# A new hand-written order for all engines, a second group of rows kept in DRAM, a first segment cut in two, and pooled sums on two engines

## The chip, the cores and the metric

One core of a Trainium2 chip runs the whole program. The metric is the device time in microseconds of one execution; lower is better. Five engines work side by side, each through its own queue in program order: TensorE (PE, with its weight loads PEld), VectorE (DVE), ScalarE (ACT), GpSimd (POOL) and SyncE (SP), which issues all DMAs here.

## What is computed

Three stages over 4608 tokens (8 batches of 576) with 512 features (8 heads of 64): attention against keys and values that are averaged over groups of 8 positions, an expert with SoLU and layer norm (512 to 1024 to 512), and an expert with SiLU (512 to 2048 to 512). The two experts' weights arrive as 64-bit floats.

```python
k_p = k.reshape(B, H, 72, 8, D).mean(axis=3)
v_p = v.reshape(B, H, 72, 8, D).mean(axis=3)
scores = scale * (q @ k_p.T)
attn = exp(scores - max(scores));  attn = attn / (sum(attn) + 1e-09)
x = attn @ v_p                                   # (4608, 512)
h = x @ w_in                                     # (4608, 1024)
sm = exp(h - max(h));  solu = h * sm / (sum(sm) + 1e-09)
ln = (solu - mean(solu)) / sqrt(var(solu) + 1e-06) * g_ln
x = ln @ w_out                                   # (4608, 512)
h = x @ w_in2                                    # (4608, 2048)
out = (h / (1 + exp(-h))) @ w_out2               # (4608, 512)
```

## The kernel before

Tokens go in 36 tiles of 128. Matrix products are made from pairs of reduced-precision operands, a high part and a low part (`fp32r`), with three matmuls for each product; the projection of the first expert and both products of the second run by a seven-product scheme for 2x2 blocks (Strassen-Winograd), whose block sums and differences are made on VectorE, ScalarE and GpSimd.

**The scripted part.** Attention, the first expert and the start of the second are issued in an order that is written out by hand: `SCRIPT` (lines 61 to 216) is a string of words, and `run` (line 1462) walks through it. A word names a generator and its arguments, and each occurrence runs that generator to its next `yield`; a suffix `/1`, `/2`, `/3` puts the step on VectorE, ScalarE or GpSimd instead of its default (`pick`, line 275). As every engine works in program order, this string fixes the order of all five queues. The words are:

- `L`, `l`: load a block of w_in as 64-bit floats; turn it into 32 bits and split it (lines 1333 and 1322). The conversion (`convert`, line 287) takes two ScalarE steps, of which the second can be on VectorE, and one VectorE step (line 307). `w` (`keep_f32`, line 326) converts a block of the second expert's weights (w2) in the same way and stores it in DRAM; there are 32 blocks. `o` (line 1383) does the first expert's second matrix, with all its sums and splits, in four calls.
- `k`, `v`, `r` (lines 381, 412, 440): load rows of keys and values, sum them over 8 positions (lines 393, 425, 453, all on VectorE), then scale or split them into small operand tiles. Loads go to three row buffers in turn.
- `q`, `S`, `X`, `T`, `a`: load a tile of queries, its scores and their maximum, the softmax (exponentials on ScalarE, products with the reciprocal on GpSimd or VectorE), transposes by TensorE and their splitting, and the attention products (`attend`, line 593). `a` works on segments of tokens: 256, 320, 320 and 256 for each two batches (`segments`, line 221).
- `H`, `M`, `E`, `Z`, `N`: hidden products of a tile (three matmuls of 512 columns each, eight words a tile), their row maximum (line 656), exponentials and sums, normalization, and transposes into a ring of six tiles (`norm_T`, line 705).
- `R`, `D`, `P`: the projection operands of a group of four tiles, the weight blocks that come from DRAM, and the seven products of the group (24 matmuls of 256 columns each), whose results go to DRAM (`x2d`). Groups are taken in the order of `LAST` (line 37): 1 to 7, then 0, then 8. Group 0's rows are normalized before the projection weights are ready; `norm_T` stores them in DRAM (`lnd`, line 722), and `u` (`reload_n`, line 725) fetches them back near the end.
- `c`, `d`: close the attention's and the hidden part's buffers and make the second expert's first tokens and weights in their place. `f` (`first_pair`, line 1058): its first seven products, 42 matmuls.

`W` issues matmuls whose result is not used.

**Behind the script** the second expert's first half runs in windows (`window`, line 1093; `product`, line 1036, matmuls at line 1043), with the conversions of its operands placed in numbered slots, and then its second half (`product2`, line 1275, matmuls at line 1286), with its operands made nine products ahead.

## Time and profile before

| | |
|---|---|
| median of 3 runs | 1294.44 us (1293.19 to 1296.17) |
| profiled execution | 1291.54 us, its span 1289.5 us |
| granted TensorE clock, mean | 0.989 |
| TensorE, VectorE, ScalarE, GpSimd busy | 96%, 79%, 62%, 36% |
| DMA | 304 MB, 236 GB/s on average |

The span runs from the first to the last instruction. A busy TensorE is not TensorE at its peak, since matmuls overlap and their ends are modelled. The granted clock tells which share of full speed the throttle allowed. The scripted part ends with the last projection at 586.7 us; the hand-over to the windows lasts to 606.2, the windows to 941 and the second half to the end. Lines are named by their number in the kernel before. In a group of instructions, `out<-in` are the program's tile names, and the figures are the sum of busy time, the mean of one in ns, and the idle time ahead of them with what ended it.

### The profile page before, as it was taken

To read this page: it belongs to the slowest core of one execution; us is meant where nothing else is said; L and a number is where in the kernel's file an instruction comes from. 1 tells how busy PE (TensorE), PEld (TensorE's weight loads), DVE (VectorE), ACT (ScalarE), POOL (GpSimd) and SP (SyncE) were. 2 spreads that over 40 slices of the span, in tenths; PEclk is the share of its full clock that TensorE was granted. 3 is DMA by queue.
4 is the path that set the end of the run, shared out by engine and by line. 5 is a ranking of instruction groups with operands and counts; after the bars stand their busy time and mean duration, and the time that the engine had idled before them with its cause. 6 is when DMAs were issued, how large, how long until landed. Compare 5 with 4: busy or idle time off the path is not lost.

```text
span 1289.5 us, 21677 instructions
## 1 busy us (share of the span) xinstructions
PE 1244.0 (96%) x7276; PEld 1134.2 (88%) x7276; DVE 1016.6 (79%) x1689; ACT 795.8 (62%) x1965; POOL 461.6 (36%) x623
## 2 busy tenths in 40 slices
PE   7788999999999999898999999999999999999999
PEld 6677778899899998898999999999988888888888
DVE  6888998998887789898766677656479887969776
ACT  6788987675465645444767677676645445554544
POOL 4777775555645645523224433333030000000000
PEclk8899999999999999999999999999999999999999
DMA  9777688766323341544778688666999988788683
GB/s 328 219 251 237 196 281 305 234 232 197 107 87 106 107 164 58 180 159 168 264 276 302 254 299 332 247 230 222 339 331 403 356 285 268 256 272 273 196 283 142
DMA packets 133167, 304.47 MB, mean 236 GB/s; under 512 B 11936, under 2 KB 56992, under 8 KB 131520
## 3 DMA queue, kind: packets, MB, share of 16 engines
q1 hardware_dynamic: 133056, 303.09, 68.1%
q8 instruction: 57, 0.93, 0.3%
q14 instruction: 54, 0.44, 0.1%
HBM read 213.91 MB, written 89.13 MB: 235 GB/s over the span
## 4 chain that ended last, share of the span: by engine, by line
PE 52%; DMA 1%; DVE 1%; issue 0%; ACT 0%; DVEq 0%; SPq 0%; ACTq 0%
PE op L1286 27%; PE m L1043 25%; DMA gd<-gb 1%; DMA w2r<-w2if 0%; DVE w2r L837 0%; PE xq L785 0%; DVE np L287 0%; DVE xo L793 0%; DVE gb L1054 0%; ACT gt L1266 0%; DVE t L837 0%; DVE wt L872 0%; DVE np L282 0%; DVE wt L837 0%; DVE w2s L837 0%
## 5 line engine op out<-in xcount | busy, mean ns | idle before, releaser
L1043 PE MATMUL m<-t,w2s 128*128 128x384 f32 x2016 | 352.6, 335 | 4.2 <-DVE gb L1054 2.1
L1043 PEld LDWEIGHTS m<-t,w2s 128*128 128x128 f32 x2016 | 350.7, 188 | 5.7 <-DVE gb L1054 2.7
L1286 PE MATMUL op<-gt,w2o 128*128 128x512 f32 (+1 forms) x1680 | 345.2, 368 | 0.0
L1286 PEld LDWEIGHTS op<-gt,w2o 128*128 128x128 f32 x1680 | 292.7, 189 | 52.4
L1266 ACT ACTIVATE gt<-gr 128x512 fp32r<-128x512 f32 (+1 forms) x240 | 139.9, 588 | 142.5 <-PE op L1286 58.9
L837 DVE TENSOR_TENSOR gt<-gr,gt 128x512 fp32r<-128x512 f32 (+1 forms) x240 | 154.6, 650 | 60.9 <-ACT gt L1266 57.4
L643 PE MATMUL hp<-w1ih,xTh 128*128 128x512 f32 x288 | 119.6, 415 | 7.3 <-DVE e L668 4.5
L785 PE MATMUL xq<-np,w1p 128*128 128x256 f32 x864 | 113.5, 284 | 1.3 <-DVE np L287 1.0
L643 PE MATMUL hp<-w1ih,xTl 128*128 128x512 f32 x288 | 114.1, 396 | 0.4 <-DVE xTl L287 0.4
L643 PE MATMUL hp<-w1il,xTh 128*128 128x512 f32 x288 | 113.6, 394 | 0.0
L785 PEld LDWEIGHTS xq<-np,w1p 128*128 128x128 f32 x864 | 107.0, 189 | 3.9 <-DVE np L287 1.7
L513 ACT ACTIVATE pr<-sp,st 128x72 f32<-128x72 f32 x288 | 88.2, 329 | 23.2 <-DVE st L504 19.2
L785 PE MATMUL xq<-np,w1o 128*128 128x256 f32 x648 | 86.7, 286 | 5.1 <-DVE np L287 3.7
L785 PEld LDWEIGHTS xq<-np,w1o 128*128 128x128 f32 x648 | 81.8, 192 | 7.8 <-DVE np L287 4.1
L287 POOL TENSOR_TENSOR np<-lnr,np 128x512 fp32r<-128x512 f32 x46 | 62.2, 1356 | 49.7 <-DVE np L282 28.8
L837 DVE TENSOR_TENSOR gr<-gr 128x512 f32<-128x512 f32 (+1 forms) x120 | 79.8, 667 | 0.2
L837 POOL TENSOR_TENSOR tt<-x2r 128x768 f32<-128x768 f32 x22 | 43.5, 1979 | 99.3 <-DMA x2r<-x2d 60.4
L643 PEld LDWEIGHTS hp<-w1ih,xTh 128*128 128x128 f32 x288 | 55.1, 191 | 18.3 <-DVE e L668 3.4
L287 DVE TENSOR_TENSOR np<-lnr,np 128x512 fp32r<-128x512 f32 x80 | 64.6, 815 | 4.4 <-ACT np L280 2.7
L666 ACT ACTIVATE e<-hp,ls 128x1024 f32<-128x1024 f32 x36 | 40.1, 1115 | 45.2 <-DVE ls L656 40.4
L643 PEld LDWEIGHTS hp<-w1ih,xTl 128*128 128x128 f32 x288 | 54.7, 190 | 13.3 <-DVE xTl L287 1.0
L280 ACT ACTIVATE np<-lnr 128x512 fp32r<-128x512 f32 x69 | 43.0, 630 | 36.1 <-PE xq L785 18.0
(177 smaller groups left out, 2225.7 us busy)
## 6 DMA issues: line engine op xcount, KB each, us to landing
w2o<-wod SPq DMA_DIRECT2D x50, 768.0 KB, 6.5
w1o<-w1od SPq DMA_DIRECT2D x54, 512.0 KB, 4.2
...
```

Of the source, the lines that this page charges most:

```text
L280: eng.activation(dst, src, AF.Copy)
L287: pick(1).tensor_tensor(lo, src, hi.bitcast(F32), op=ALU.subtract)
L513: nc.scalar.activation(pr[:, g, h], sv[:, g, h], AF.Exp, bias=st[:, 0, g, h : h + 1], accum_out=st[:, 1, g, h : h + 1],)
L643: nc.tensor.matmul(hp[:, f], l, r, start=(n == 1 and m == 0), stop=(n == KC and m == 2))
L666: nc.scalar.activation(e, hp, AF.Exp, bias=nm, accum_out=sm)
L785: nc.tensor.matmul(hq[:, b], w[:, k, l], t[:, k % 2, r], start=(b == k == i == 0), stop=(k == 3 and i == 2), skip_group_check=True,)
L837: eng.tensor_tensor(dst, a, b, op=ALU.subtract)
L1043: nc.tensor.matmul(to, wt[:, a, o : o + P], tk[:, b, k], start=(start and k == 0 and m == 0), stop=(k == 1 and m == 2), skip_group_check=n ...
L1266: nc.scalar.activation(ring[m][:, 0], src, AF.Copy)
L1286: nc.tensor.matmul(acc[c, x][d], w[:, l, P * d : P * d + P], t[:, r], start=(first and f == i == 0), stop=(f == NF - 1 and i == 2), skip_g ...
```

## The change

1. `SCRIPT` is a new string, all words from first to last in a new order, with 2881 instead of 2859 words. Of the 32 w2 conversions (`w`), 27 were begun ahead of tile 15's row maximum and the last ahead of tile 19's; now 15 are begun ahead of tile 15's and the last ahead of tile 30's. The key loads come earlier in the opening. The `f` words stand behind the last projection matmul; two of their seven products stood ahead of it.
2. `SPILL = 2`: group 1 is treated as group 0 was. Its rows go to DRAM (four stores of 0.52 MB more), are fetched back by two reloads of 1.05 MB more, and `LAST` takes it fourth: 2, 3, 4, 1, 5, 6, 7, 0, 8. The first projection is that of group 2, behind hidden tile 12 instead of tile 11.
3. The first segment of 256 tokens is two of 128. In the order the attention products of the first (`a0`) stand behind tile 0's transposes and ahead of tile 1's.
4. `pool_sum` lets a word put a pooled sum on GpSimd, as three halving adds in place; 19 of the 80 sums are there. `scaled` and `pick` do the same for the scaling and the splitting of pooled keys and values, which can now be on any of three engines.

```diff
-LAST = (1, 2, 3, 4, 5, 6, 7, 0, 8)
+SPILL = 2
+LAST = (2, 3, 4, 1, 5, 6, 7, 0, 8)
...
 SCRIPT = """
-L0,1 L0,0 W14 L0,2 k0,0 v0,0 k0,2 L0,3 q0 l0,1 L1,0 l0,1 l0,1 W29 l0,1 l0,0 l0,1 l0,2 q1
-l0,0 l0,0 k0,0 L1,1 l0,0/3 k0,1 k0,1 k0,1 v0,0 v0,2 k0,0 k0,0 l0,2/1 W6 l0,2 v0,1 l0,2/3
-r0,0 W4 k0,3 l0,2/3 k0,2 l0,3 L1,3 l0,3/1 k0,3 l0,3 k0,3 k0,2 L1,2 k0,2 S0 k1,0 l0,0 l0,3 S0
...
-R8,2 P8,2 N34 R8,5 d P8,2 P8,1 D8,4,0 R8,6 f R8,6 D8,4,1 R8,6 R8,6/3 R8,6 f f P8,2 R8,6/3 d
-P8,6 P8,2 f R8,4 d P8,6 R8,7 P8,5 P8,6 R8,7/1 d d P8,5 D8,2,0 R8,7 R8,7/3 R8,7 d R8,7 P8,7
-R8,3/1 D8,2,1 R8,3 R8,3 P8,5 R8,3/3 P8,7 P8,3 P8,7 P8,7 R8,4/1 P8,3 R8,4 R8,4/3 R8,4/1 R8,4
-P8,4 d d d P8,4 P8,3 P8,3 f P8,4 d P8,4 f f f f f f f f f f f
+L0,0 k0,0 W14 L0,2 k0,2 q0 L0,1 q1 q6 W6 l0,0 L0,3 W29 k0,0 k1,0 l0,0/1 k0,1 l0,2 k0,1/3
+k0,1/1 l0,0 l0,2/1 k0,0/1 k0,0 l0,2 k0,2 l0,2 k0,3 k0,2 k0,2/1 k0,3/1 k0,3/3 S0 l0,1 S0 q2
+k1,1 S1,1 l0,0/1 X0 v0,0 l0,1/1 v0,2 l0,2 X0 W4 r0,0 S1,1 L1,3 X0 X0 l0,0 v1,0 X1 l0,1 X1
...
+N35 R8,2 P8,2 R8,5 R8,6/3 P8,2 D8,4,0 R8,6 D8,4,1 R8,6 R8,6/3 R8,6 d R8,6 P8,6 P8,1 c P8,6
+R8,7 d P8,2 P8,5 R8,7 d P8,2 c d P8,5 d D8,2,0 R8,7/3 R8,7 P8,6 R8,7 R8,3 D8,2,1 R8,7 P8,7 d
+d d d P8,7 R8,4 R8,3 R8,3 R8,3 P8,3 R8,4 R8,4/3 R8,4 P8,5 R8,4 P8,3 d R8,4 P8,4 P8,7 P8,7
+P8,4 P8,3 P8,3 f P8,4 d P8,4 f f d d f f f c f f f f f f f f f f
 """
...
-        for a, n, b in ((0, 256, 0), (256, 320, 0), (576, 320, 1), (896, 256, 1)):
+        first = ((0, 256, 0),) if j else ((0, 128, 0), (128, 128, 0))
+        for a, n, b in first + ((256, 320, 0), (576, 320, 1), (896, 256, 1)):
...
-    lnd = [dram.tile([P, FC1, 2 * P], F32, tag=f"lnd{h}", name="lnd") for h in range(2)]
+    lnd = [dram.tile([P, FC1, 2 * P], F32, tag=f"lnd{h}", name="lnd") for h in range(2 * SPILL)]
...
+    def pool_sum(dst, raw):
+        if pick(1) is nc.vector:
+            nc.vector.reduce_sum(dst, raw, axis=AX)
+            return
+        for n in (4, 2, 1):
+            to = raw[:, :, 0:n] if n > 1 else dst.rearrange("p (k o) -> p k o", o=1)
+            nc.gpsimd.tensor_tensor(to, raw[:, :, 0:n], raw[:, :, n : 2 * n], op=ALU.add)
+
+    def scaled(n, dst, src, scale):
+        if pick(n) is nc.scalar:
+            nc.scalar.activation(dst, src, AF.Copy, scale=scale)
+        else:
+            pick(n).tensor_scalar(dst, src, scale, 0.0, op0=ALU.mult, op1=ALU.add)
...
-        nc.vector.reduce_sum(kp[:, p], raw, axis=AX)
+        pool_sum(kp[:, p], raw)
...
-            nc.gpsimd.tensor_tensor(lo, vp[r], hi.bitcast(F32), op=ALU.subtract)
+            pick(3).tensor_tensor(lo, vp[r], hi.bitcast(F32), op=ALU.subtract)
...
     def norm_T(t):
         e = v_t.pop(t)
-        o = (t if t < NTILE - GT else t + GT) % TRING * P
+        g, i = divmod(t, GT)
+        o = (t if g < SPILL else (SPILL + LAST.index(g)) * GT + i) % TRING * P
...
-        if t < GT:
+        if g < SPILL:
             nc.sync.dma_start(lnd[t // 2][:, :, t % 2 * P : t % 2 * P + P], ring_t[0][:, :, o : o + P])
...
-    def reload_n(h):
-        o = (NTILE - GT + 2 * h) % TRING * P
-        nc.sync.dma_start(ring_t[0][:, :, o : o + HW], lnd[h])
+    def reload_n(g, h):
+        o = ((SPILL + LAST.index(g)) * GT + 2 * h) % TRING * P
+        nc.sync.dma_start(ring_t[0][:, :, o : o + HW], lnd[2 * g + h])
```

## Rows read from the trace of the kernel before

**Rows 1.** The page's part 1: busy us (share of the span) xinstructions, by engine.

```profile
PE 1244.0 (96%) x7276; PEld 1134.2 (88%) x7276; DVE 1016.6 (79%) x1689; ACT 795.8 (62%) x1965; POOL 461.6 (36%) x623
```

**Rows 2.** The chain that ended last, in time: start us, us, what.

```profile
588.58 6.14 DMA w2r<-w2if
...
606.17 316.86 PE m L1043 x1818
...
941.29 345.00 PE op L1286 x1680
```

**Rows 3.** Windows: stretch, length, busy (x) PE PEld DVE ACT POOL, PEclk, DMA share, GB/s.

```profile
0.00:52.10 52.10, 37.06 (x230) 33.13 (x230) 38.61 (x65) 35.35 (x134) 26.43 (x44) 0.90 0.85 285
52.10:182.00 129.90, 114.63 (x620) 94.42 (x620) 116.23 (x226) 110.93 (x399) 98.36 (x190) 0.96 0.75 239
182.00:332.50 150.50, 148.62 (x1031) 136.18 (x1032) 135.94 (x246) 100.56 (x292) 87.13 (x131) 1.00 0.68 228
332.50:478.20 145.70, 145.19 (x984) 132.93 (x983) 118.64 (x212) 79.29 (x250) 83.01 (x126) 1.00 0.35 111
...
535.00:586.70 51.70, 47.29 (x372) 45.97 (x372) 46.75 (x69) 22.26 (x38) 17.03 (x17) 0.97 0.54 172
586.70:606.20 19.50, 15.44 (x87) 14.48 (x85) 13.77 (x16) 7.91 (x16) 8.26 (x5) 0.99 0.60 212
```

**Rows 4.** Timeline, VectorE: row maxima of tiles 0 and 11: start us, us, instruction.

```profile
52.14 1.22 DVE L656 TENSOR_REDUCE ls<-hp 128x1 f32<-128x1024 f32 x1
...
182.03 1.23 DVE L656 TENSOR_REDUCE ls<-hp 128x1 f32<-128x1024 f32 x1
```

**Rows 5.** Windows as in rows 3: first and last half-clock stretch ahead of 605 us.

```profile
22.20:29.10 6.90, 5.37 (x25) 5.35 (x26) 5.96 (x12) 5.41 (x21) 4.80 (x6) 0.51 1.04 393
...
544.40:548.00 3.60, 2.97 (x14) 3.00 (x15) 2.50 (x4) 3.41 (x6) 3.33 (x5) 0.53 0.23 90
```

**Rows 6.** Groups by line and form, and line 307's spread (ns min/median/max).

```profile
L307 DVE SCALAR_TENSOR_TENSOR w<-w,tail 128x512 int32<-128x512 int32 x48 | 38.5, 803 | 9.7 <-ACT tail L303 8.8 <-ACT w L299 0.3
L307 DVE SCALAR_TENSOR_TENSOR w<-w,tail x48: 672/691/2650, 6.0 to 356.0; 128x512 int32<-128x512 int32 x48
L393 DVE TENSOR_REDUCE kp<-raw 128x72 f32<-128x576 f32 x28 | 20.7, 745 | 4.7 <-DMA raw<-kT 3.9 <-POOL kbd L406 0.8
L425 DVE TENSOR_REDUCE vp<-raw 128x64 f32<-128x512 f32 x28 | 18.6, 673 | 3.1 <-DMA raw<-vm 3.1
L287 DVE TENSOR_TENSOR xTl<-av,xTh 128x128 fp32r<-128x128 f32 x24 | 6.0, 279 | 0.9 <-ACT xTh L280 0.9
L287 DVE TENSOR_TENSOR np<-lnr,np 128x512 fp32r<-128x512 f32 x80 | 64.6, 815 | 4.4 <-ACT np L280 2.7 <-POOL np L284 0.8
L287 DVE TENSOR_TENSOR ptl<-pm,pth 128x512 fp32r<-128x512 f32 x32 | 21.9, 686 | 0.6 <-ACT pth L280 0.2
L689 POOL TENSOR_TENSOR ls<-ls 128x1 f32<-128x1 f32 x36 | 10.6, 294 | 2.8
L525 POOL TENSOR_TENSOR pb<-pr,st 128x512 f32<-128x512 f32 x24 | 25.8, 1074 | 25.2 <-DVE st L521 23.2 <-ACT kbd L402 1.8
```

**Rows 7.** Timeline of the opening: the last key sums, first scores, first hidden product.

```profile
13.24 1.40 DVE L393 TENSOR_REDUCE kp<-early 128x72 f32<-128x576 f32 x2
...
15.38 1.15 PE L494 MATMUL sp<-kbd,q 128*128 128x144 f32 x8
...
38.79 0.50 PE L643 MATMUL hp<-w1ih,xTh 128*128 128x512 f32 x1 [2.55 <-ACT xTh L280]
```

**Rows 8.** Waits: engine, line, releaser: us in total, times, longest us.

```profile
DVE vlp L453 <- DMA raw<-vl: 4.9, 3, 3.5
...
SPq L722 <- ACT lnr L280: 6.0, 1, 6.0
```

**Rows 9.** Timeline, VectorE and GpSimd from 33 to 36 us.

```profile
33.24 2.65 DVE L307 SCALAR_TENSOR_TENSOR w<-w,tail 128x512 int32<-128x512 int32 x1
...
34.07 1.27 POOL L287 TENSOR_TENSOR w1il<-w,w1ih 128x512 fp32r<-128x512 f32 x1
```

More of the change, by code (lines that the diff above doesn't have):

```diff
@@ new lines @@
+E18 D4,1,1 Z18 Z18 H19,0,0 N17/1 N17 P3,3 H19,0,1 w20 R4,1/1 P3,3 w16 T23 R4,1 H19,1,0 X26
+w16/1 R4,1/1 X26 T23 w21 H19,0,2 w16 r5,1/2 R4,1/3 w19 N17/1 H19,0,3 w16 w19 r6,1 k7,3
+H19,1,1 X26 r5,1 w22 H19,1,2 R3,4 X26 w19 H19,1,3 X26 R3,4/3 T23 P4,1 M19 v6,3 Z18 X26 S27
+X25 E19 T23 R3,4/3 P3,4 Z18/2 q30 E19 X26 w19 u1,0 N16 P3,4 w20/1 k7,3/2 v6,3 T23/1 w23 T23
+v7,0 X26 T24 w20 H20,0,0 E19 P3,4 Z19 Z19 T24 H20,1,0 X25/1 H20,1,1 w21 S27 Z19 H20,1,2
+T24/1 P4,1 R4,2/1 Z19/2 k7,3 T24 r6,0 r6,1/3 X27 N18 T24/1 v6,3 v7,1 N19 T24 X25 v7,2
@@ new lines @@
+D1,1,0 R4,7/3 R4,7 w24 r7,0 H22,0,0 w25 R1,1 R4,7/3 H22,1,0 E21 R4,7 Z21 Z21 P4,7 S29 P4,5
+Z21 P4,7 R1,1 r6,1/1 a11 v7,3/3 Z21/2 P4,7 H22,1,1 a11 H22,0,1 Z20/2 P4,3 R4,4/3 a11 a11 a11
+R1,1/3 H22,1,2 a11 a11 H22,0,2 H22,1,3 H22,0,3 R4,4 R4,4/3 R1,1/3 R4,4 w22 N20 w26 T25
+R4,4/3 P4,7 T25 T25/1 P4,4 T25 T25 u1,1 P4,3 w22 D1,1,1 X27 M22 w22 q32 N20/1 N20 P4,4 N20
+E22 P1,1 P4,4 X28 P4,4 X28/1 N21 X28 T26 E22 N21 P1,1 R1,2/1 E22 R1,2 R1,2 Z22 T26 H23,0,0
+R1,2 H23,1,0 X27 T25 w24 T26/1 P1,2 X29 R1,5 Z22 T26 R1,5 H23,0,1 T26/1 X29 D1,4,0 R1,5
@@ new lines @@
+R6,5/3 a14 M28 N27 R6,5/3 S35 N27 a14/1 E28 a14 a14 R6,6/3 a14 S35 P6,5 E28 X35 X35 P6,5
+a14/1 D6,2,0 E28 a14 R6,7/3 Z28 X34 a14 a14 D6,2,1 Z28 R6,6/1 H29,1,0 a14 T31/1 R6,3 Z28
+H29,1,1 w28/1 T31 X35 H29,1,2 w28 X35 R6,3 T32 H29,0,1 H29,0,0 R6,6/3 R6,6 R6,4 R6,6 a14
+H29,1,3 T32 T32 R6,3 T32 H29,0,2 T32 X35 R6,6/3 w30 T32 H29,0,3 X35 T31/1 T31 T33 M29 Z28
+T33 P6,6 T33/1 R6,3/3 T33 T33 E29 P6,6 E29 P6,3 R6,7/3 P6,6 H30,0,0 R6,7/3 R6,7 P6,5 R6,7
+D7,1,0 w28 a15 H30,1,0 E29 R6,7 P6,7 w30 X35 Z29 w30 P6,7 r7,1 r7,1 Z29 H30,0,1 P6,7 R6,4
@@ new lines @@
+X34 H30,0,3 H30,1,1 Z29 R6,4 H30,0,2 T33 v7,3/1 N28 Z29 P6,3 N28 r7,1/2 X35 N28 X34 D7,1,1
+a15 N28/1 R6,4/3 N29 a15/1 N29 a15 a15 a15 H30,1,2 u0,0 R6,4/3 a15/1 P6,7 a15 a15 a15 a15/1
+a15 a15 a15 T34 H32,0,0,1 P6,3 T34 T34/1 P6,3 H30,1,3 T34 T34 T35 H32,1,0,1 M30 T35
+H32,0,1,1 T35/1 E30 H32,1,1,1 T34 T35 H32,0,2,1 T35 E30 a16 N29 H32,1,2,1 T35 E30 a16 N29/1
+Z30 Z30 H31,0,0 R6,4 a16/1 a16 a16 a16 H31,0,1 a16 a15/1 R7,1/1 a16 a16 a16 R7,1/3 R7,1
+a16/1 a16 a16 a16 H31,1,0 a16 H31,1,1 a16 Z30 a15 c H31,0,2 c c H31,0,3 H31,1,2 c H31,1,3 c
@@ L401, in prep_k @@
             if b <= 1:
-                nc.scalar.activation(
-                    kb[r, p, e * SP : (e + 1) * SP], kp[r, p], AF.Copy, scale=SCALE
-                )
-            else:
-                nc.gpsimd.tensor_scalar(
-                    kb[r, :, e * SP : (e + 1) * SP], kp[r], SCALE, 0.0, op0=ALU.mult, op1=ALU.add
-                )
+                scaled(2, kb[r, p, e * SP : (e + 1) * SP], kp[r, p], SCALE)
+            else:
+                scaled(3, kb[r, :, e * SP : (e + 1) * SP], kp[r], SCALE)
             done("k", b)
@@ L424, in prep_v @@
         vp = vp_t[b]
-        nc.vector.reduce_sum(vp[:, p], raw, axis=AX)
+        pool_sum(vp[:, p], raw)
         done("vp", b)
@@ L452, in prep_v_rest @@
         vp = vr_t[b]
-        nc.vector.reduce_sum(vp[:, g], raw, axis=AX)
+        pool_sum(vp[:, g], raw)
         done("vr", b)
@@ L466, in prep_v_rest @@
         for j in range(4):
-            nc.gpsimd.tensor_scalar(
-                vls[i][:, j // 2 :: 2, (j % 2) * D : (j % 2 + 1) * D],
-                vh.bitcast(F32), mask[:, j : j + 1], 0.0, op0=ALU.mult, op1=ALU.add,
-            )
+            to = vls[i][:, j // 2 :: 2, (j % 2) * D : (j % 2 + 1) * D]
+            scaled(3, to, vh.bitcast(F32), mask[:, j : j + 1])
             done("v", b)
```

269 lines of the change are left out of this document (124 added, 145 removed).

## The prediction, made before the result was known

> **What bounds the kernel now.** The page's first lines come first: TensorE is busy 96% of the span, VectorE 79%, ScalarE 62%, GpSimd 36% [rows 1]. The chain of work that ended last says where: from 606.2 us on it is matmuls of the second expert without a gap worth naming, 317 us of line 1043 and then 345 us of line 1286 [rows 2]. No line of that part is changed and its operands come in the same order, so the 683 us behind 606.2 stay as they are. The change can only act ahead of that point.
>
> There I read busy time by stage, cut at the row maxima of the hidden tiles (word M, line 656), since each marks the same progress in both orders [rows 3, 4]. Tile 0's maximum stands at 52.1 us, tile 11's at 182.0; tile 35's is where the stage from 535.0 begins. From tile 0 to tile 11 TensorE is busy 114.6 of 129.9 us (88%), VectorE 116.2 (89%), ScalarE 110.9 (85%), GpSimd 98.4 (76%): no engine is full, and the vector work is what the others queue behind. From 182.0 to 332.5 VectorE has 90% and TensorE 98.8%; from 332.5 to 478.2 VectorE falls to 81% and TensorE has 99.7%: there TensorE is the bound and VectorE has 27 us to spare. Behind tile 35 TensorE drops again, to 91%, and in the hand-over from 586.7 to 606.2 it idles 4.1 us.
>
> So the time is lost in the first 182 us (30.3 us of idle TensorE: 15.0 and 15.3) and at the end of the scripted part (4.4 and 4.1 us). Idle costs twice: in stretches among the gaps the granted clock is 0.51 to 0.53, the 1.2 GHz level instead of 2.4, once for 6.9 us and otherwise for about 3.5; six such stretches lie ahead of 605 us, the first and the last of which are shown, five of them in the first 122 us [rows 5].
>
> **The change, part by part.** Nearly the same instructions run; where they stand is new. I counted the words of both orders ahead of tile 11's maximum, because up to there neither order has a projection and both have the same 96 hidden products.
>
> *w2 conversions later.* Word w has run its vector step (line 307) 13 times ahead of that point before, 6 times after: seven fewer at 0.803 us are 5.6 us of VectorE [rows 6], and two ScalarE steps go with each. *Pooled sums on two engines.* VectorE has 58 of the sums ahead of that point before and 46 after: 12 at 0.71 us (the mean of 0.745 and 0.673) take off 8.5 us [rows 6]. Eleven stand on GpSimd instead, as three halving adds. The trace has no such add. From the nearest rows three adds cost between 0.9 us (three times 0.294, the smallest two-input form) and 3.2 us (three times 1.074, 128x512) [rows 6]; I take 1.9, near the middle, since their 288, 144 and 72 elements lie between. *What comes back to VectorE:* 23 small scalings and splittings of pooled keys and values that GpSimd or ScalarE had, at about 0.3 us (nearest row 0.279 [rows 6]), 6.8 us, and 0.2 of other differences. Net VectorE has 7.1 us less ahead of tile 11, 2.1 of it ahead of tile 0. GpSimd has 2.5 us more, since much that was its own is moved away. Means overstate, because neighbours overlap at their ends: my list gives 167.7 us of VectorE ahead of tile 11 where rows 3 show 154.8, so I scale by 0.92. Between tile 0 and tile 11 that is 5.0 x 0.92 = 4.6 us of work, and at a VectorE share of 89% the stage becomes **5.1 us** shorter. Bounds: 0 (the waits are chains, not load) and 10 us (twice that, if ScalarE's relief counts too).
>
> *Opening.* The first scores wait for all pooled keys of the first batch: the last two sums start at 13.24 us, the scores at 15.38 [rows 7]. Before, 3.28 MB are asked for up to and with the second key load (three blocks of w_in at 0.52, keys 0.59, values 0.52, keys 0.59), after 2.23 MB (two blocks, two key loads). 1.05 MB at 285 GB/s [rows 3] are **3.7 us**. Behind the scores the first segment is one tile, so the first hidden product, at 38.79 us before [rows 7], no longer waits for a second softmax. Against that, values are asked for later and there are 16 more attention matmuls. Bounds 0 and 6 us; I take 3.7.
>
> *Middle.* What left the first part must be done later. From tile 11 up to the place that is reached at 332.5 us now, the counted VectorE work is even (153.5 before, 151.1 after); in the stage behind it rises by 7.3 x 0.92 = 6.7 us, so from 118.6 to 125.3 of 145.7 us, 86%. At 90% TensorE idled 1.2%, at 81% 0.3% [rows 3]: the loss is 0 to 1.3 us, and I take **1.0**.
>
> *Second group through DRAM.* Four more stores of 0.52 MB in the first part and two reloads of 1.05 MB in the middle, where the DMA engines are busy 35 to 68% [rows 3]. In the first part nine w2 blocks fewer are read (0.52 MB) and written (0.26), which more than pays for the stores. SyncE's queue could suffer: a store waits for its copy, once 6.0 us before, and key, value and q loads stand behind it. There are now eight such places instead of four. VectorE waited for value rows up to 3.5 us at a time [rows 8], so this costs 0 to 3 us; I take 0, as row buffers are asked for three ahead. The reloads are asked for two tiles and half a tile ahead of their readers; 1.05 MB at 285 GB/s are 3.7 us, half a tile some 6.
>
> *End.* Behind tile 35 the two orders have 42.1 and 34.7 us of TensorE work left by my count, and vector work moves with it. No product of the first pair, instead of two, stands ahead of the last projection matmul; their twelve matmuls, at 316.86/1818 = 0.174 us, move 2.1 us of work into the hand-over, where TensorE waits for w2 rows (6.14 us to land, then sums) [rows 2] and idles 4.1. There they cost nothing; in front of it they are gained if TensorE sets the pace, and not if VectorE does. Bounds -2.1 and +1 (a later w2 load); I take **-1.0**.
>
> **A rule that speaks against it.** A vector step with a median of 0.691 us once took 2.65, with GpSimd instructions running through it [rows 6, 9]. The Trainium skill ("SBUF — State Buffer", section "Who interferes with whom") says that a vector instruction with two inputs in SBUF and a GpSimd one that reads SBUF exclude each other for a whole instruction, and that a vector reduce does not contend, so exchanging reduces for GpSimd adds would cost vector time. That one row agrees. By the rule at its worst the time would be 1306.5, by the median of the row 1285.6; the first is among the rivals.
>
> **Sum**, against the profiled execution (1291.54 us, a span of 1289.5 and 2.04 around it): -5.1 - 3.7 + 1.0 - 1.0 = -8.8, so 1282.7. The median of the runs is 2.9 us above that execution, and I put the forecast on the median: **1285.6**.
>
> **Rivals.**
> *Held vector work* (slower). If each GpSimd sum kept VectorE waiting for its whole 1.9 us, eleven of them would give back 20.9 us: 1306.5. It decides, nothing gained, from 42% of that. Against it: line 307 lies 0.112 us above its median, 5.4 us over 48, and line 287 with two SBUF inputs 0.129 above its form with one, 10.3 over 80 [rows 6]; 16 us over some 320 of GpSimd work [rows 3] are 5%, so 1 us here. Chance 0.06.
> *Middle becomes vector-bound* (slower). If the stretch from 332.5 to 478.2 ran at the 88% of the first part, its 145.2 us of TensorE work would take 165, 19 more: 1285.6 + 18 = 1304. It decides from a TensorE share of about 94%. For it: VectorE at 89% went with 88% in the first part. Against: at 90% it went with 98.8% in the next [rows 3]. Chance 0.14.
> *Larger gain.* Lighter ScalarE and VectorE let the softmax chains run with fewer gaps, so that half of the 15.3 us idle goes besides: 1278.0, and up to 1.75 us less for each half-clock stretch that goes too. Chance 0.20.
> *Given back.* VectorE's whole scripted load is the same (536.8 and 536.1 us by my count), and it ends the stage again: 1294.4. For it its 90% behind tile 35; against it its slack in the middle [rows 3]. Chance 0.15.
>
> **How the numbers follow.** Forecast 0.45, larger 0.20, given back 0.15, middle 0.14, held 0.06. What a measurement of this kernel can tell from no change is about 0.2%, 2.6 us. Faster: the forecast but for its upper edge (0.42), larger (0.20) and a little of given back: 0.64. Same: most of given back and that edge: 0.16. Slower: middle and held: 0.20. The range runs from 1274.5, the larger gain with two half-clock stretches fewer, to 1300, most of the middle rival's way.
>
> **What would show it.** Tile 0's maximum near 48 us, tile 11's near 173; first scores near 12; VectorE near 86% between 320 and 470 us with TensorE still above 98%; the last 683 us unchanged. The prediction is wrong if tile 11 comes no earlier (then chains, not load, set the first part), if TensorE idles in the middle, or if vector instructions with two SBUF inputs grow by more than 5% on average.

## The result, and the profile after

The changed kernel takes 1282.23 us in the median of 4 runs (1279.98 to 1283.69), the kernel before 1293.82 (4 runs): a ratio of 0.9907, 95% interval 0.9885 to 0.9929. The forecast was 1285.6. The profiled execution took 1281.28 us, with a span of 1279.5; that is 10.3 us less than the profiled execution before.

Part 1 of the page of the changed kernel, as in [rows 1]:

```profile
PE 1242.0 (97%) x7292; PEld 1131.2 (88%) x7292; DVE 1016.8 (79%) x1719; ACT 794.1 (62%) x1949; POOL 480.7 (38%) x655
```

VectorE's sum over the span is unchanged (1016.6 before); GpSimd has 19 us more. What changed is where the work stands. The windows of the changed kernel, cut at tile 0's, 11's and 35's maxima and the last projection as in [rows 3], and between them at 320 and 463, where TensorE has done 99% and 98% of the work (columns of its matmuls, warm-up left out) that it had done at 332.5 and 478.2 before (columns as there: stretch, length, busy and count of PE, PEld, DVE, ACT, POOL, granted clock, DMA share, GB/s); the last row is a stretch of the opening, as in [rows 5]:

```profile
0.00:50.00 50.00, 38.85 (x247) 35.17 (x247) 34.79 (x74) 30.47 (x123) 25.49 (x48) 0.86 0.80 272
50.00:168.80 118.80, 108.78 (x616) 90.41 (x617) 110.96 (x228) 106.42 (x379) 96.21 (x196) 1.00 0.69 211
168.80:320.00 151.20, 147.78 (x1001) 134.31 (x1000) 139.44 (x248) 107.35 (x332) 102.20 (x151) 1.00 0.77 251
320.00:463.00 143.00, 140.57 (x975) 128.71 (x974) 119.96 (x221) 78.69 (x224) 85.04 (x120) 1.00 0.49 156
...
534.30:575.80 41.50, 37.43 (x294) 34.95 (x293) 38.03 (x55) 21.10 (x35) 17.53 (x19) 1.00 0.45 147
575.80:594.80 19.00, 16.89 (x99) 16.57 (x97) 14.60 (x19) 8.92 (x18) 8.72 (x5) 1.00 0.61 219
26.00:40.00 14.00, 9.53 (x36) 8.46 (x37) 12.38 (x28) 9.02 (x29) 10.66 (x18) 0.51 0.87 320
```

Tile 0's row maximum comes at 50.0 us instead of 52.1, tile 11's at 168.8 instead of 182.0 [rows 4] (timeline; start us, us, instruction, in brackets the idle time ahead of it and what ended it):

```profile
168.79 1.23 DVE L669 TENSOR_REDUCE ls<-hp 128x1 f32<-128x1024 f32 x1 [0.29 <-PE hp L656]
```

So the 10.0 us of span are made up like this:

| stretch | before | after | difference | forecast |
|---|---|---|---|---|
| start to tile 0's maximum | 52.1 | 50.0 | -2.1 | -3.7 |
| tile 0's to tile 11's maximum | 129.9 | 118.8 | -11.1 | -5.1 |
| tile 11's maximum to the last projection | 404.7 | 407.0 | +2.3 | +1.0 (middle) |
| hand-over to the windows | 19.5 | 19.0 | -0.5 | -1.0 (end) |
| windows and second half | 683.3 | 684.7 | +1.4 | 0 |

Nearly everything lies between tiles 0 and 11, and there ahead of tile 5's maximum, which comes 51.8 us after tile 0's instead of 64.1; from there to tile 11's the new order takes 67.0 instead of 65.8 (windows of both halves, the kernel before first):

```profile
52.10:116.20 64.10, 56.10 (x302) 46.89 (x302) 54.00 (x107) 54.37 (x205) 51.28 (x101) 0.95 0.78 241
116.20:182.00 65.80, 58.53 (x318) 47.54 (x318) 62.23 (x121) 56.56 (x194) 47.08 (x89) 0.97 0.72 237
50.00:101.80 51.80, 47.64 (x268) 40.00 (x268) 48.53 (x98) 47.51 (x175) 43.74 (x88) 1.00 0.62 185
101.80:168.80 67.00, 61.14 (x349) 50.41 (x350) 62.43 (x131) 58.91 (x205) 52.47 (x109) 1.00 0.73 230
```

In the first half VectorE works 5.5 us less and idles 6.8 less, and some 34 matmuls, with the work of other engines that belongs to them, now stand behind tile 5; in the second half VectorE's work is the same. Over both halves VectorE works 5.3 us less (116.2 to 111.0; forecast 4.6) and idles 5.8 us less (13.7 to 7.8); TensorE's granted clock is 1.00 throughout where three stretches at the 1.2 GHz level stood before. The questions for the experiments were how much of the 11.1 us the lighter load is worth, how much the clock, and how much the order by itself; and why the opening gave little.

### The profile page after: what moved, and what is told of

It reads as the page before. It is cut to its first block, busy times and chain, and to the rows that moved or that the text cites. A ratio compares the mean times of both kernels' runs of the same rounds, so it can differ in the third digit from the quotient of the medians.

```text
span 1279.5 us, 21818 instructions
## 1 busy us (share of the span) xinstructions
PE 1242.0 (97%) x7292; PEld 1131.2 (88%) x7292; DVE 1016.8 (79%) x1719; ACT 794.1 (62%) x1949; POOL 480.7 (38%) x655
## 4 chain that ended last, share of the span: by engine, by line
PE 52%; DVE 2%; DMA 1%; issue 0%; SPq 0%; ACT 0%; DVEq 0%; ACTq 0%
PE m L1057 27%; PE op L1300 24%; DVE gr L851 1%; PE xq L799 1%; DMA gr<-gd 1%; DVE gt L851 1%; SPq L1217 0%; DVE w2s L851 0%; DVE ob L1333 0%; DVE t L851 0%; DVE np L292 0%; ACT gt L1280 0%; ACT np L285 0%; DVE lnr L759 0%; DVE xo L807 0%
## 5 line engine op out<-in xcount | busy, mean ns | idle before, releaser
L1068 DVE TENSOR_TENSOR gb<-m,u 128x384 f32<-128x384 f32 x48 | 26.7, 556 | 49.1 <-ACT u L1124 31.9
L1068 DVE TENSOR_TENSOR ga<-m,u 128x384 f32<-128x384 f32 x47 | 26.1, 555 | 49.3 <-PE m L1057 49.0
```

Source lines behind the costliest of these rows:

```text
L1068: eng.tensor_tensor(dst, a, b, op=ALU.add)
```

## The experiments

In the kernels below, most line numbers are about a dozen lower than in the kernel they come from, and each ratio is to runs of the kernel before beside them. Landmarks and stages are those of one profiled execution each. The kernel before had medians of 1292.0 to 1293.8 us in these rounds, so a difference between medians of two rounds is uncertain by about 2 us. "The stage" is tile 0's to tile 11's row maximum.

### Load and order apart: a square of four kernels

**Load taken out of the old order.** In `keep_f32` and `convert` of the kernel before, six of the conversions between the two maxima skip two steps:

```diff
-        w = yield from convert(src, by_act)
+        w = yield from convert(src, by_act, out=n in (2, 4, 6, 8, 10, 12))
...
+        if out:
+            yield
+            yield
+            return w
         tail = stage.tile([P, 512], I32, tag="sign", name="tail", bufs=1)
```

> The kernel before without the second and third step (the tail and the vector step of line 307) of six w2 conversions (blocks 2, 4, 6, 8, 10, 12), all between tile 0's and tile 11's maxima; their loads, first steps and stores stay, so those blocks hold wrong numbers. It is the load that the change moves out of this stage, taken out in place with no change of order: 4.8 us of VectorE, about 4 of ScalarE. Load: the stage goes from 129.9 to 124.5 to 126 us, the time from 1293 to 1287 to 1289. Order: the three waits of TensorE for value sums stay, and the stage stays at 128 to 130 us, the time within 2.5 us of the kernel before.

Measured: 1293.08 us, a ratio of 1.0002 (0.9988 to 1.0016): no change. Its window for the stage:

```profile
51.92:179.88 127.96, 112.80 (x620) 93.63 (x620) 110.27 (x219) 108.24 (x393) 96.47 (x189) 0.97 0.75 242
```

VectorE's sum over the stage is now that of the changed kernel (110.3 and 111.0), ScalarE's and GpSimd's are within 2 us, and the stage takes 128.0 us, 9.2 more than there. But the load is not gone from the same places: most of the six conversions stand behind tile 5, where the change took nothing off VectorE's sum (the two halves of this run, as above):

```profile
51.92:116.20 64.28, 54.68 (x302) 45.77 (x302) 52.76 (x104) 53.26 (x202) 49.89 (x100) 0.97 0.76 239
116.20:179.88 63.68, 58.12 (x318) 47.86 (x318) 57.51 (x116) 54.98 (x191) 46.58 (x89) 0.97 0.74 246
```

Ahead of tile 5 VectorE is 1.2 us lighter here and 5.5 in the changed kernel; behind it 4.7 us taken out gave 2.1. The 1.9 us that it won are lost again by tile 35's maximum (535.2 us, 535.0 in the kernel before). The expectation by order was right.

**Load put back into the new order.** The changed kernel with six words `Y`, one each behind the row maxima of tiles 1, 3, 5, 7, 9 and 10 or a few words later:

```diff
+    def extra(n, i=0):
+        t = stage.tile([P, 4, P], I32, tag="sign", name="extra", bufs=1)
+        x = ident.bitcast(U32).rearrange("p (o n) -> p o n", o=1).to_broadcast([P, 4, P])
+        nc.scalar.activation(t, x, AF.Copy, bias=FLOOR, scale=TAIL3)
+        y = ident.bitcast(I32).rearrange("p (o n) -> p o n", o=1).to_broadcast([P, 4, P])
+        nc.vector.scalar_tensor_tensor(t, y, 3, t, op0=ALU.logical_shift_left, op1=ALU.bitwise_or)
+        yield
```

> The changed kernel with six extra pairs of steps between tile 0's and tile 11's maxima, one ScalarE step and one VectorE step of the size of a w2 conversion's second and third (128x512), on constants, with a result that nothing reads: 4.8 us of VectorE and 4 of ScalarE, what w2_steps_out_on_before took out of the kernel before. Order kept, load put back. If load and order are two separate causes, the stage grows as it shrank there, by about 1.9 us, to 120 to 121.5, and the time to 1283 to 1286. If the new order has taken the waits away so that the load now counts in full (the prediction's term, 5.1 us), it grows to 123 to 124.5 and the time to 1285 to 1288. If the load doesn't matter in the new order, it stays within 1 us of 118.8.

Measured: 1288.07 us, a ratio of 0.9964 (0.9951 to 0.9976), which lies outside the changed kernel's interval. Its window for the stage, and the six VectorE steps:

```profile
51.05:176.16 125.11, 112.16 (x622) 92.50 (x622) 115.44 (x234) 109.38 (x384) 97.42 (x196) 0.99 0.65 199
```

```profile
L1441 DVE SCALAR_TENSOR_TENSOR extra<-ident,extra x6: 691/812/1056, 63.4 to 171.0; 128x512 int32<-128x512 int32 x6
```

VectorE's 115.4 us are those of the kernel before (116.2), and the stage takes 125.1: 6.3 us more for 4.8 us of work. The expectation had three cases; this is the one in which the load counts in full, and slightly more. A part of it may be the clock: behind the fifth step stands a half-clock stretch (window), in a stage that ran at 1.00 throughout in the changed kernel.

```profile
157.70:161.10 3.40, 3.40 (x11) 2.69 (x10) 3.34 (x11) 2.82 (x8) 2.82 (x8) 0.50 1.02 406
```

(Tile 0's maximum, ahead of any extra step, came 1.05 us later in this profile, so about 1 us of the 5.8 between the medians is scatter or belongs elsewhere.) The square:

| stage, us (VectorE busy) | old order | new order |
|---|---|---|
| load of before | 129.9 (116.2) | 125.1 (115.4) |
| light load | 128.0 (110.3) | 118.8 (111.0) |

Read down, the load is worth 1.9 us in the old order, all of it given back later, and 6.3 in the new one, of which 4.8 are left at tile 35's maximum (counted from tile 0's). Read across, the new order is worth 4.8 us with the heavy load and 9.2 with the light one. "New order" stands here for all of the change but this load, the cut segment and the second group in DRAM included; none of these was run alone. And the load is equal as a sum over the stage, not place by place. So neither the order at the old load nor the load taken out of these conversions in the old order gives the 11.1; what the same load would have been worth if taken out ahead of tile 5 in the old order was not run.

**The sums alone.** The changed kernel with `pool_sum` reduced to its first form:

```diff
     def pool_sum(dst, raw):
-        if pick(1) is nc.vector:
-            nc.vector.reduce_sum(dst, raw, axis=AX)
-            return
-        for n in (4, 2, 1):
-            to = raw[:, :, 0:n] if n > 1 else dst.rearrange("p (k o) -> p k o", o=1)
-            nc.gpsimd.tensor_tensor(to, raw[:, :, 0:n], raw[:, :, n : 2 * n], op=ALU.add)
+        nc.vector.reduce_sum(dst, raw, axis=AX)
```

> The changed kernel with all 80 pooled sums on VectorE (19 had been on GpSimd, 11 of them ahead of tile 11's row maximum, 3 of these ahead of tile 0's); every word stays where it is. Load (VectorE's amount of work sets the pace of the first part): 8 sums at 0.71 us between tile 0's and tile 11's maxima are 5.2 us of VectorE after the factor 0.92, so that stage goes from 118.8 to about 124 us, tile 0's maximum comes 0 to 2 us later, and the time is 1286 to 1289. Held vector work (the rival of the prediction: the adds of GpSimd keep VectorE waiting, 1.5 us for each sum): 11 sums give back 16.5 us and cost 7.8, so the stage shortens and the time is about 1274. Order (a few waits between engines set the pace, not the amount): the stage stays within 1.5 us of 118.8 and the time within 2 us of 1282.2.

Measured: 1285.37 us, a ratio of 0.9948 (0.9928 to 0.9968).

```profile
50.62:170.71 120.09, 108.96 (x616) 90.51 (x617) 115.01 (x236) 106.59 (x379) 84.61 (x172) 1.00 0.68 208
```

The stage grows by 1.3 us and the next tile by 2.3 more, so 3.6 us up to tile 12's maximum, with 4.1 us of VectorE time added in the stage, and the kernel by 3.1 (medians). The load expectation was too high for the stage and right in sign; the order expectation holds up to tile 11 and fails one tile later. At tile 35's maximum, counted from tile 0's, 3.6 us are left. So work on VectorE has no single price in the new order either: at tile 11, 4.1 us cost 1.3 here, and 4.5 cost 6.3 above. That VectorE would be held by GpSimd's adds is refuted: without them the kernel is slower, not 8 us faster.

### What in the old order cost the time

In the kernel before, TensorE's longest waits in the stage (engine, line, releaser: us in total, times, longest) were for results of the softmax and of the SoLU step:

```profile
PE pm L553 <- POOL pb L525: 5.9, 3, 3.4
PE hp L643 <- DVE e L668: 4.5, 7, 1.3
PE sp L494 <- ACT pr L513: 3.8, 1, 3.8
```

The one of 3.4 us goes back to a value sum: the reciprocal of a softmax stands behind it in VectorE's queue, and its rows are late (timeline of the kernel before):

```profile
114.69 1.48 DVE L453 TENSOR_REDUCE vlp<-raw 96x64 f32<-96x512 f32 x2 [3.54 <-DMA raw<-vl]
117.46 0.79 PE L553 MATMUL pm<-ident,pb 128*128 128x128 f32 x4 [3.39 <-POOL pb L525]
```

In the changed kernel VectorE waits for no value rows in this stage, and TensorE's longest entries are less than half as large:

```profile
PE hp L656 <- DVE e L681: 1.9, 4, 0.7
PE pm L566 <- POOL pb L538: 1.6, 2, 1.4
```

**Three places mended in the old order**, by moving words alone:

```diff
-... S4 r1,0 l1,3/3 r1,1 v2,0 k2,1 ... k2,3 S4 H0,0,3 ...
+... S4 S4 r1,0 l1,3/3 r1,1 v2,0 k2,1 ... k2,3 H0,0,3 ...
...
-... r2,0 E1 o0/3 a1 a1 a1 v3,0 v2,3 ...
+... v2,3 E1 o0/3 a1 a1 a1 v3,0 r2,0 ...
...
-... r4,0 X11 o2 H5,1,2 r4,1 q13 ... M5 ... N4 N4 E5 X10 ...
+... X11 o2 H5,1,2 q13 ... M5 ... N4 N4 E5 r4,0 r4,1 X10 ...
```

> The kernel before with three places of its order changed and no work added, taken out or given to another engine: the row maximum of the scores of tile 4 goes ahead of the two value sums (line 453) and the key sum that it stood behind; two value sums ahead of tile 1's vector step change places; the two value sums that stood just ahead of tile 5's row maximum go behind that tile's next vector step. At these three places VectorE waited 1.4, 0.9 and 3.5 us for value or key rows, and TensorE then idled 3.8 us at 52.9, 2.2 at 68 to 70 and 3.4 at 117.5, each time with a half-clock stretch behind. Order: the idle shrinks to below 1.5 us at each place and at least two of the three half-clock stretches go, so that the stage from tile 0's to tile 11's maximum takes 121 to 125 us instead of 129.9 and the time is 1284 to 1289 (before: 1292 to 1294). Load (the amount of VectorE's work sets that stage): nothing is lighter, so 128.5 to 130.5 us and a time within 2 us of the kernel before.

Measured: 1290.63 us, a ratio of 0.9972 (0.9956 to 0.9988).

```profile
50.87:178.84 127.97, 113.08 (x615) 92.61 (x613) 116.70 (x226) 110.75 (x393) 95.34 (x186) 0.96 0.76 242
```

The stage is 1.9 us shorter with the same load, less than half of what was expected. The wait of 3.4 us did go, the middle one shrank from 2.2 to 1.7, and of the 3.8 us 2.4 are left, which now lie ahead of tile 0's maximum (timeline):

```profile
49.45 2.00 PE L483 MATMUL sp<-kbd,q 128*128 128x144 f32 x8 [2.38 <-ACT pr L502]
```

Still, tile 5's row maximum came 60.0 us after tile 0's instead of 64.1. But tile 11's came 68.0 after tile 5's instead of 65.8, so half was given back, and half-clock stretches remain (the first one, now twice as long, and a new one at 80.5 us; 0.96 on average, as before). The waits for rows are a part of what the order costs, not the whole; unlike the load, most of what was won here stayed (tile 35's maximum 2.8 us earlier, 1.3 of it from ahead of tile 0's).

**Whole conversions out, and all three together.** In `keep_f32` of the kernel before:

```diff
+        if n in (2, 4, 6, 8, 10, 12):
+            for _ in range(4):
+                yield
+            kept["w"] += 1
+            yield
+            return
         w = yield from convert(src, by_act)
         nc.sync.dma_start(dst, w)
+        if 20 <= n < 26:
+            m = 2 * n - 38
+            nc.sync.dma_start(w2if[m // 4][:, m % 4], w)
```

> The kernel before without the whole conversion of the w2 blocks 2, 4, 6, 8, 10 and 12 at their places (loads, three steps and stores); their homes in DRAM are filled later with other blocks' rows, so the second expert computes with wrong numbers. Against w2_steps_out_on_before (127.96 us from tile 0's to tile 11's maximum) it also takes away 3.1 MB of loads, 1.6 MB of stores, and the waits of six loads and six stores on SyncE's queue. Queue and transfers: the stage falls well below 127.96, to 122 to 125 us. Engines alone: 126.5 to 128 us (six more steps of ScalarE less). Whether the time follows (up to 7 us) or is given back behind tile 11, as it was for w2_steps_out_on_before, is the second question; I expect that half or more is given back, time 1288 to 1292.

The second kernel has this, the three places above and the stores behind loads (next).

> The kernel before with the edits of sums_behind_on_before, stores_behind_on_before and w2_blocks_out_on_before together (the last leaves out the whole conversion of six w2 blocks at their places, and the second expert computes with other blocks' rows). If the causes stand in for each other, so that each alone only uncovers the next wait, the three together shorten the stage by more than the sum of the three alone, to about 119 to 121 us, near the 118.8 of the changed kernel. If they are independent, it shortens by their sum, about 1.9 and what the other two give. If it stays above 124 us, something else in the new order makes up the rest.

The first took 1294.12 us (1.0008, 0.9991 to 1.0026), with 126.75 us for the stage; the three together 1294.48 (1.0017, 1.0002 to 1.0032), with 125.68.

```profile
51.35:178.10 126.75, 113.84 (x620) 94.13 (x620) 110.31 (x219) 104.67 (x383) 96.12 (x187) 0.96 0.66 207
```

With 3.1 MB of loads less the stage is 1.2 us shorter than with the two steps out, so transfers and SyncE's queue are not the main cost, as I had half expected; and it was given back at the next projections (tile 12's maximum 30.8 us behind tile 11's instead of 26.2). The three together stay 6.9 us above the changed kernel's stage: by the expectation, something else in the new order makes up that rest. But the third part did harm when run alone (next), so the three are no bound on what waits for rows and stores cost. The kernel without the conversions but with a store more for six later blocks is no clean test of what is given back behind tile 11.

**Stores behind loads.** The last of the three parts, alone; seventeen stores were moved (13 of w2 blocks, 4 of normalised tiles), as these:

```diff
-... v3,3 N1 w0 H3,0,0 ... q11 v4,0 ...
+... v3,3 N1 H3,0,0 ... q11 w0 v4,0 ...
...
-... X8 S9 N1 w4 ... H5,0,3 v4,3 E4 ...
+... X8 S9 w4 ... H5,0,3 v4,3 N1 E4 ...
```

> The kernel before with the stores of w2 blocks and of normalised tiles that lie between tile 0's and tile 11's maxima moved on SyncE's queue behind the next four row loads (keys, values, queries), where the buffers allow it; nothing else is moved and no work changes. In the kernel before, stores waited at the head of that queue for their data for 15.5 us (w2 blocks, 6 times) and 6.0 us (a normalised tile, once, from about 100.6 to 106.7 us, with the value loads behind it for which VectorE then waited 3.5 us at 114.7). SyncE's queue (rows come late because stores block their loads): VectorE's waits for value rows fall from 4.5 us to below 1.5, and the stage goes from 129.9 to 125 to 127 us, time 1288 to 1291. Rival (the rows come late because the DMA engines are busy, 0.67 to 1.07 of the time there, or the rows are not the limit): 129 to 131 us, time within 2.5 us of the kernel before.

It made the kernel slower: 1316.28 us (1.0186, 1.0164 to 1.0209), the stage 153.1 us. The row that says why is among the waits of ScalarE in that stretch:

```profile
ACT w L288 <- DMA w2if<-w: 26.9, 9, 5.4
```

A conversion's first step writes one of three buffers that a store empties; with the store issued later, ScalarE waited for it nine times. These stores had to stand where they stood.

**All w2 conversions moved.** They were placed by the TensorE work done ahead of them in the other kernel. In the changed kernel this packs thirteen of their steps into one spot:

```diff
-... a0 X2 l1,1 l1,1/1 ...
+... a0 X2 w1 w2 w1 w0 w0 w3 w0 w0 w2 w2 w2 w4 w2 l1,1 l1,1/1 ...
```

> The changed kernel with the five steps of each w2 conversion put back to the places they had, by TensorE work done, in the kernel before: 13 instead of 6 conversions ahead of tile 11's maximum, 3 instead of 0 ahead of tile 0's. All else stays. Load: 4 more conversions between the two maxima are 3.2 us of VectorE and 5.4 of ScalarE, so the stage goes from 118.8 to 122 to 124 us; 3 more ahead of tile 0 cost 0 to 2.4 us; behind tile 11 at most 1.3 us come back. Time 1285 to 1288. Order: the stage stays within 1.5 us of 118.8, time within 2 us of 1282.2.

It took 1333.67 us (1.0315, 1.0292 to 1.0337), with tile 0's maximum at 71.7 us. TensorE waited 12.6 us for a vector step that stood behind that pack (timeline), whose conversions share the three buffers and waited for one another's stores:

```profile
56.46 0.47 PE L606 MATMUL av<-ptl,vbh 128*128 128x128 f32 x1 [12.62 <-DVE ptl L280]
```

The mirror image, with steps such as `w0` from behind `T0 v0,2` to behind `S2 T1` and the later ones further:

> The kernel before with its w2 conversions moved to the places that they have in the changed one: 6 instead of 13 ahead of tile 11's maximum (182.0 us there), none instead of 1 ahead of tile 0's. All else stays. Load: 6 fewer between the two maxima take 4.8 us off VectorE and 8 off ScalarE, so the stage goes from 129.9 to about 125 us, and the time from 1293.8 to 1288 to 1290, if the later conversions find slack behind. Order: the waits of TensorE in that stage (3.8 us at 52.9, 2.2 at 68 to 70, 3.4 at 117.5) hang on softmax steps and stay, and with them the half-clock stretches behind them: stage 128.5 to 130, time 1292 to 1295.

It took 1316.19 us (1.0177, 1.0150 to 1.0204). The stage took 133.3 us, and most of the loss lies behind it (375.3 us to tile 35's maximum, 353.0 in the kernel before). There loads on SyncE's queue waited for a conversion's row buffer, and TensorE 6.7 us for projection weights (0.9 before); the rest of the loss was not followed up (waits behind the stage, up to tile 35):

```profile
SPq L282 <- DVE tail L293: 29.6, 5, 9.8
PE xq L773 <- DMA w1o<-w1od: 6.7, 3, 3.3
```

So these two say nothing on the load, which they were made for: all engines work in program order, and a word can't be moved without what it waits for. They do show the size of the thing: one kind of word in places that don't fit costs 24 to 51 us, more than all the change brings.

### The clock

In the kernel before, TensorE ran at the 1.2 GHz level behind each of the three places in the stage where it waited longest (windows):

```profile
52.85:56.35 3.50, 3.50 (x16) 3.49 (x17) 2.51 (x5) 1.82 (x4) 3.17 (x6) 0.52 0.97 315
70.20:73.70 3.50, 3.25 (x9) 2.58 (x10) 3.50 (x9) 1.77 (x6) 3.15 (x7) 0.53 0.75 221
117.80:121.30 3.50, 3.35 (x12) 2.19 (x11) 3.34 (x7) 3.50 (x14) 2.28 (x5) 0.51 0.54 184
```

> The kernel before with 68 extra 128x128 matmuls of the identity (28, 8, 7 and 25, at about 0.12 us each) placed on TensorE where it idles in the stage from tile 0's to tile 11's maximum: ahead of the scores at 52.9 us, of the transposes at 68.8, of the hidden products at 70.4 and of the transposes at 117.5. They compute nothing that is used and end about when the awaited operand comes. Clock: the granted clock stays at 1.00 behind these places (before: 0.50 to 0.53 for 3.4 us each), and the stage shortens by up to 1.7 us for each, 3 to 5 us in all: 125 to 127 us instead of 129.9, the time 1288 to 1291. Clock without effect (the other engines set the pace behind each wait as well): the clock is 1.00, but the stage stays at 129 to 131 us and the time at that of the kernel before.

```diff
+... X4 W28 S5 ... v2,3 W8 T5 ... v2,3 W7 H2,0,1 ... w5 W25 T10 ...
```

Measured: 1296.11 us (1.0020, 1.0009 to 1.0031), and the stage 131.96 us at a granted clock of 1.00:

```profile
51.45:183.41 131.96, 121.34 (x731) 103.06 (x729) 115.28 (x226) 110.86 (x399) 98.93 (x190) 1.00 0.72 235
```

My fillers were twice as long as meant: a word of `W28` is 56 matmuls, not 28 (timeline).

```profile
48.42 6.41 PE L1420 MATMUL idle<-ident 128*128 128x128 f32 x56
```

They held TensorE up by about 2.6, 2.8 and 2.0 us at the three places beyond the waits there, 7.4 in all, and the stage grew by 2.1. The 5.3 us between are what three stretches at full clock would give back (three times half of 3.5 us), but slack could give it too. The run does not tell the clock's price apart.

### The opening

In the changed kernel the first scores stand at 14.6 us, not near 12. All keys are summed and in place by 12.1; TensorE is still busy with the script's own `W` matmuls, which stand ahead of the scores in its queue. In the kernel before, whose line comes first, they ended together with the keys, so it could not be seen there which of the two the scores waited for (timeline; SPq is SyncE's issue of a DMA):

```profile
1.86 13.68 PE L1431 MATMUL idle<-ident 128*128 128x128 f32 x106 [1.86 <-POOL ident masks.py:199]
...
1.86 12.92 PE L1445 MATMUL idle<-ident 128*128 128x128 f32 x98 [1.86 <-POOL ident masks.py:199]
11.81 0.25 POOL L398 TENSOR_SCALAR kbd<-kp 64x72 f32<-64x72 f32 x1 [3.81 <-DVE kp L388]
14.61 2.13 PE L507 MATMUL sp<-kbd,q 128*128 128x144 f32 x16
...
5.82 0.33 SPq L403 DMA_DIRECT2D raw<-kT  x1
15.79 0.33 SPq L491 DMA_DIRECT2D q<-qT  x1
16.63 0.91 SPq L435 DMA_DIRECT2D early<-vm  x2
...
29.85 2.26 PE L507 MATMUL sp<-kbd,q 128*128 128x144 f32 x8 [6.54 <-DMA q<-qT]
```

And SyncE issues nothing from 6.2 to 15.8 us. The next load in its queue, tile 2's queries, needs a buffer; there are three, tile 6's queries were loaded into one of them at the start, and the next comes free with the first scores. The loads of keys and values stand behind it. The DMA engines fall silent for 3.4 us, with a share of 0.03 and 6 GB/s (window, columns as above):

```profile
13.20:16.60 3.40, 3.40 (x32) 3.40 (x31) 0.81 (x2) 0.01 (x1) 0.00 (x0) 1.00 0.03 6
```

Two words were exchanged for a test: `q2` at the start in place of `q6`, and `q6` behind `q3`.

```diff
-... q0 L0,1 q1 q6 W6 ... S0 q2 k1,1 ... q3 l0,1 ...
+... q0 L0,1 q1 q2 W6 ... S0 k1,1 ... q3 q6 l0,1 ...
```

> The changed kernel with the query rows of tile 2 asked for at the start, where those of tile 6 had been, and those of tile 6 behind those of tile 3; all else stays. SyncE's queue (its load of tile 2's rows waits from 6.15 to 15.79 us for a row buffer that the scores of tile 0 free; the loads of keys and values stand behind it, and the DMA engines lie idle from about 13 to 16.6 us): without that wait the value rows are asked for near 7 us, the DMA engines do not fall idle, TensorE's 6.5 us wait for tile 3's rows goes or shrinks below 3 us, tile 0's maximum comes at 45 to 47 us instead of 50.0, and the time is 1277 to 1280. Rival (the opening is set by the vector work on keys, values and w_in, or by the bytes, and the wait is covered): tile 0's maximum stays within 1 us of 50.0 and the time within 2 us of 1282.2.

Measured: 1278.74 us, a ratio of 0.9895 (0.9868 to 0.9921).

```profile
5.87 1.62 SPq L391 DMA_DIRECT2D raw<-kT  x2
8.61 1.00 SPq L423 DMA_DIRECT2D early<-vm  x2
26.91 1.82 PE L495 MATMUL sp<-kbd,q 128*128 128x144 f32 x8 [2.90 <-ACT pr L514]
```

The value rows are asked for 8 us earlier and the 6.5 us wait is gone, but tile 0's maximum comes at 48.07, only 1.9 us earlier: the next wait, for exponentials, stood close behind, and a half-clock stretch stayed (10.2 us instead of 13.7). I had expected 45 to 47. Against the changed kernel the intervals overlap; the medians differ by 3.5 us, by the ratios it is 1.6, and the opening accounts for 1.9.

On top of it, matmuls of the identity in the two waits that were left:

```diff
+... l1,3 W22 S3 ... l1,2 W11 a0 ...
```

> The kernel q2_before_q6 (1278.7 us, tile 0's maximum at 48.07) with 33 extra matmuls of the identity that nothing uses: 22 ahead of tile 3's scores, where TensorE idled 2.9 us, and 11 ahead of the first attention matmul, where it idled 1.7. Clock: the stretch at half clock there (from about 28 to 36.5 us) goes, the attention matmuls and hidden products behind run in half the time, and tile 0's maximum comes 1.5 to 3 us earlier, at 45 to 46.5; time 1275.5 to 1277.5. Rival (VectorE, busy above 90% from 17 to 35 us, sets the opening): the clock is 1.00, and tile 0's maximum stays within 0.7 us of 48.1, the time within 1.5 us of 1278.7.

Measured: 1276.26 us, a ratio of 0.9858 (0.9839 to 0.9876), below the changed kernel's interval. The same stretch that stood at 0.51 in the changed kernel:

```profile
26.00:40.00 14.00, 12.98 (x100) 11.97 (x99) 12.73 (x27) 11.25 (x40) 12.28 (x19) 1.00 0.76 278
```

Here, too, the fillers ran longer than the waits: tile 3's scores come at 28.3 us instead of 26.9. Nevertheless tile 0's maximum is 0.75 us earlier (47.3). So up to 2.1 us came back in between, by the full clock or out of slack; the run can't tell them apart, and 0.75 us is less than the 1.05 by which tile 0's maximum differed between two profiles of one opening (50.0 and 51.05, above). It lies between the two expectations: VectorE, busy 12.7 of 14 us, is close to the bound in the opening. This kernel has the lowest median of all that were run, 2.5 us below the one without the fillers, but the two intervals touch (0.9868 and 0.9876).

## Why the prediction was right, and where it was not

**The total.** The sum said -8.8 us against the profiled execution, and it was -10.3. The other 1.9 us of the 3.4 between forecast and median come from putting the forecast on the median, 2.9 above the profiled execution; after the change that distance was 1.0. That the sum is so close is in good part luck: the stage from tile 0 to tile 11 gave 6.0 us more than forecast, and the other four stretches 4.8 us less together.

**Tile 0 to tile 11 (-5.1, measured -11.1, outside its bounds of 0 to 10).** The count of work was good (VectorE 5.3 us lighter, where 4.6 had been reckoned), and in the new order as much load counts about as the step had it: 6.3 us when put back, 4.8 of them left at tile 35. What failed is the sentence that no engine is full and the vector work is what the others queue behind, taken as true of the order before. In that order as much load, taken out mostly behind tile 5, was worth 1.9 us and nothing at the end. The new order is worth 4.8 us more at an equal sum of load, and this term was missing; the waits of [rows 8] were read as a risk of the change and put at nothing instead of being followed back as a cost of the order before. The three places account for 1.9 of it in the old order. The rest could not be pinned to single words; all of the gain lies ahead of tile 5, where VectorE's idle time fell by 6.8 us.

**Pooled sums on GpSimd.** Taken at 1.9 us, with bounds 0.9 and 3.2; measured, for a key sum, 0.80 + 0.45 + 0.39 = 1.64. Groups by line and form of the changed kernel:

```profile
L292 DVE TENSOR_TENSOR np<-lnr,np 128x512 fp32r<-128x512 f32 x83 | 65.1, 792 | 10.7 <-ACT np L285 7.2 <-POOL np L289 2.5
L392 POOL TENSOR_TENSOR raw<-raw 128x288 f32<-128x288 f32 x5 | 4.0, 800 | 0.2
L392 POOL TENSOR_TENSOR raw<-raw 128x144 f32<-128x144 f32 x5 | 2.3, 451 | 0.4
L392 POOL TENSOR_TENSOR kp<-raw 128x72 f32<-128x72 f32 x5 | 2.0, 393 | 0.4
```

**Held vector work (rival, 0.06).** It did not happen: VectorE's form with two SBUF inputs takes 792 ns on average where it took 815 [rows 6], and 804 with the sums back on VectorE; taking the adds away made the kernel slower. The Trainium skill ("SBUF — State Buffer", section "Who interferes with whom") has such a vector instruction and a GpSimd one exclude each other; no run here shows a loss from the 57 adds.

**Opening (-3.7, measured -2.1).** The step that failed is "The first scores wait for all pooled keys of the first batch", with the bytes up to the second key load as its price. The keys did come 3.5 us earlier (12.1 instead of 15.6). But TensorE's queue held 98 matmuls ahead of the scores up to 14.6 us, which the script's first line shows, and behind the scores the row buffers blocked SyncE's queue. The prediction looked at that queue for stores only. With the queries exchanged tile 0's maximum came 4.1 us earlier than in the kernel before, near the size that had been forecast, but not in the way: the first scores stood at 15.3 us in that profile (15.4 before), and all of it was won behind them.

**Middle and end (0 in sum, measured +1.8).** The middle was under-sized, and idle of TensorE there was one of the prediction's own signs of being wrong: TensorE idles 3.4 us between 168.8 and 320 us and 2.4 in the stretch behind, 1.9 and 0.5 before [rows 3], so 3.5 us more where 1.0 had been put; up to the last projection 2.3 of it is left. VectorE is at 92% and 84% there (forecast near 86% for the second). The rival "middle becomes vector-bound" has this mechanism but at a fifth of its size. The hand-over shows -0.5 of the -1.0:

```profile
594.78 3.59 PE L1057 MATMUL m<-t,w2s 128*128 128x384 f32 x13 [2.11 <-DVE gb L1068]
```

One wait of 2.1 us is left where three of 1.2, 0.7 and 2.1 stood.

**Second group through DRAM (0).** It was not run by itself. The trace of the changed kernel speaks for the term: of the eight stores one kept SyncE's queue waiting, for 1.6 us, VectorE waited for no value rows in the stage, and no computing engine waited for the rows of group 1 to come back.

**Behind the hand-over (0, measured +1.4).** Nothing of it is changed; from tile 35's maximum to the end the profiles of the old order scatter between 753.2 and 756.1 us, those of the new between 744.0 and 746.0, so 1.4 us of one profile can't be told from scatter.

**Given back (rival, 0.15)** fits what load did in the old order: the kernel with the two steps out had gained 1.9 us at tile 11 and nothing at tile 35. (So had the one with whole conversions out, which is no clean test.) In the new order it did not happen. The case "larger gain" (1278.0) is the one the stage itself went towards: VectorE's idle time nearly halved, TensorE's fell by a third (15.3 to 10.0 us), and three half-clock stretches went.
